# Attention scores of two heads in the row halves of the PE array, with the mask as matmuls of its own

## The chip, the cores and the metric

The kernel runs on one core of a Trainium2 chip. The metric is the device time of one execution in microseconds (us). Kernels are compared with runs of the kernel before on the same chip.

Names used below: PE is the TensorE (matmuls and transposes), PEld the loading of its weights, PSUM the memory that it writes its results to, ACT the ScalarE, DVE the VectorE, POOL the GpSimd. A "pair" is two heads of one batch; there are 4 batches of 4 pairs.

## The reference, cut to what matters

```python
# q, k, v: (4, 8, 768, 64); float32
k_rep = k.reshape(B, H, 12, 64, 64).mean(axis=3)       # 12 key blocks of 64
gate  = einsum('bhsd,bhnd->bhsn', q, k_rep)            # future blocks: -1e9
top   = the 3 best blocks of each query, plus its own block
scores = where(mask by block & causal, q @ k.T / 8, -1e9)
attn   = softmax(scores) @ v
x      = attn, heads side by side                      # (3072, 512)
out    = gelu_tanh(x @ w_in) @ w_out                   # 512 -> 2048 -> 512
```

So per batch there is an attention stage (scores, exp, values) and an MLP of two layers. Most of the arithmetic is in the MLP.

## The kernel before

The kernel lists its operations with estimated durations and priorities. A small list scheduler in it fixes one order for each engine when the kernel is built. The order is static: it does not change when an instruction is late on the chip. 110 "filler" matmuls of zeros with the lowest priority stand where this plan sees the PE idle.

The block mask is folded into the score matmul. Each head has a query tile of 76 rows: 64 rows of q, then 12 rows that say which key blocks are shut. The key tile has 12 rows in which row n is a large number over the columns of block n. One matmul over 76 rows gives score plus mask:

```python
# before, cut; i: buffer of the pair, h: head of the pair
def kc(a, h):                        # one copy per head: to rows 0 to 63
    copy(eng, kT16[i][h][0:64, a * HALF:(a + 1) * HALF],
         plan.buf["wk", p, a][64 * h:64 * h + 64, 0:HALF])
...
def mask(_):                         # mask, transposed: 64 columns = 2 heads x 32
    for c in range(1, NC):
        nc.tensor.transpose(mk16[0:64, c * 128:(c + 1) * 128],
            madd[i][:, 2 * (c - 1):2 * c, :].rearrange("p a b -> p (a b)"), ident16)
def mc(h):                           # one copy per head: to rows 64 to 75
    copy(eng, qT16[i][h][64:76, 128:S], ...[32 * h:32 * h + 12, 128:S])
...
groups = [(0, 5), (1, 4), (2, 3)]    # key chunks; 896 score columns in a unit
for h in range(2):
    for gi, (ja, jb) in enumerate(groups):
        # scores into one of two PSUM tiles "wide" of 1024 columns
        nc.tensor.matmul(st[:, x:e], kT16[i][h][0:76, s0:s0 + 128],
                         qT16[i][h][0:76, ...], start=True, stop=True)
        # exp of 896 columns on ACT -> at; causal triangle on POOL
        # values: 7 matmuls of 65 columns: at (128 x 128) x [v | 1]
```

Then follow the division by the row sum (DVE), a transpose (PE), and the MLP: line 629 is its first layer (512 and 256 columns at a time), line 659 its second (512 columns). The second layer of a batch is spread over the attention stage of the next batch: the static order puts its matmuls between score and value matmuls so that the PE need not wait for the exps.

The softmax here doesn't subtract the row's maximum and nothing guards it: scores larger than these inputs give would overflow.

## Time and profile before

| | us |
|---|---|
| time, median of 2 runs | 294.15 |
| span of the profiled execution | 291.4 |
| first matmul of the MLP starts | 49.8 |
| last matmul of batch 0's first MLP layer starts | 76.0 |
| last MLP matmul starts | 287.2 |

First the head of the page: the span and the busy time of each engine.

```profile
span 291.4 us, 5960 instructions
PE 279.3 (96%) x2330; PEld 173.8 (60%) x2330; DVE 144.0 (49%) x448; ACT 191.5 (66%) x252; POOL 48.0 (16%) x119
```

The PE is nearest to its span, but the ends of matmuls in this profile are modelled, so "busy" alone proves little. The Trainium skill says the same ("Perfetto Trace Analysis" has the TensorE profile time as "a model, not a measurement"). What is recorded is the start of every matmul, and the distance from one start to the next is what the first of the two cost. In this trace these distances are nearly always 29 to 36 ns for 65 columns, 55 or 56 for 128, 108 to 110 for 256 and 215 to 220 for 512. From about 50 us on there is hardly anything else: the PE is packed, and every nanosecond that it saves or loses there goes to the total time. (TensorE: Matmul & The Clock Gate, "Wait — 56ns, not 53.3ns?", gives 55.6 and 215.7 ns for 128 and 512 columns; this trace agrees.)

Next the busy time of the engines in four stretches: up to the first MLP matmul, batch 0's first MLP layer, everything to the last MLP matmul, and the end.

```profile
core 0: us, PE busy (x) PEld busy (x) DVE busy (x) ACT busy (x) POOL busy (x), PEclk, DMA share, GB/s
0.00:49.80 49.80, 43.90 (x466) 34.12 (x467) 34.98 (x126) 34.25 (x51) 16.94 (x46) 1.00 1.13 191
49.80:76.10 26.30, 25.23 (x176) 16.07 (x174) 11.75 (x38) 16.23 (x22) 0.41 (x1) 1.00 1.17 171
76.10:287.20 211.10, 209.81 (x1693) 123.65 (x1691) 97.31 (x287) 140.46 (x179) 30.69 (x72) 1.00 0.37 73
287.20:291.40 4.20, 0.37 (x2) 0.00 (x0) 0.00 (x0) 0.58 (x1) 0.00 (x0) 0.98 0.17 62
```

The first stretch is different from the rest: there 108 of the 110 fillers run, so the PE has room, and ACT and DVE carry the copies. In the third stretch the PE is busy for 209.8 of 211.1 us.

Two pieces of the PE's timeline in the packed part, in the order start, length, engine, line, operation. One is a stretch of an attention stage (L533 scores, L571 values, L659 second MLP layer). The other is the first MLP layer (L629) with mask transposes (L472) in between.

```profile
91.40 0.55 PE L533 MATMUL wide_85<-qT_0_116,kT_0_118 76*128 76x512 f16 x3
91.78 0.38 PE L571 MATMUL bank_88<-v_114,at_1_1_1443 128*128 128x65 f16 x7
92.00 0.38 PE L659 MATMUL bank_89<-w_out_103,gT_986 128*128 128x512 f16 x1
92.22 0.55 PE L533 MATMUL wide_86<-qT_0_116,kT_0_118 76*128 76x512 f16 x3
...
136.28 0.49 PE L629 MATMUL wide_86<-xT_1428,w_in_102 128*128 128x512 f16 x2
136.70 0.47 PE L472 MATMUL bank_88<-ident_96,madd_121 128*64 128x128 f16 x5
137.10 0.71 PE L629 MATMUL wide_86<-xT_1428,w_in_102 128*128 128x512 f16 x3
```

Read the starts. The 896 score columns take 91.78 - 91.40 = 0.38 us, just their columns; the 76-row scores stand between 128-row matmuls without any gap. The mask transposes do not fit so well. Two MLP matmuls (512 and 256 columns, 0.325 us) should end 0.325 us after 136.28, but L472 starts after 0.42 us. Five transposes of 128 columns (0.28 us) take 0.40 us (24 ns of the difference lie between the first two of them). Their weights are 64 columns wide (128\*64 in the line), all others are 128 wide. So each change of tile width costs about 95 ns here, and about 110 ns with what the matmul after it loses.

### The profile page before, as it was taken

Reading aid. Unit: us, or ns where it says so; the run is one execution under the profiler, and the core shown is the slowest. Engines: PE = TensorE matmul, PEld = TensorE weight load, DVE = VectorE, ACT = ScalarE, POOL = GpSimd, SP = SyncE. Lnnn points to the kernel's source line nnn. Section 1 sums busy time; section 2 is a strip of 40 time slices with the busy share of each in tenths; the row PEclk is TensorE's granted clock in tenths of the full one; section 3 lists DMA queues with packets and bytes.
Section 4 is the critical chain, followed back from the end, with each engine's and each line's share of the span. In section 5 each row is a group of like instructions: output and inputs, shape, how many; then the busy total and the mean of one; then the engine's idle time right before and its main releaser. Section 6 shows DMA issues by size and latency. Waiting matters only on the chain.

```text
span 291.4 us, 5960 instructions
## 1 busy us (share of the span) xinstructions
PE 279.3 (96%) x2330; PEld 173.8 (60%) x2330; DVE 144.0 (49%) x448; ACT 191.5 (66%) x252; POOL 48.0 (16%) x119
## 2 busy tenths in 40 slices
PE   7998899899999999999999999999999999999994
PEld 6776667575666655656646665666557644665441
DVE  4787873138578878673676978850024410000000
ACT  3667869557799695676789976376799921664111
POOL 7023224000043220000024430000034400000000
PEclk9999999999999999999999999999999999999999
DMA  9999999999999966865822110200000101100111
GB/s 171 219 213 197 190 171 174 199 170 146 168 159 175 163 133 146 177 127 97 128 43 64 58 38 37 74 0 0 2 36 2 40 36 72 38 0 2 72 72 72
DMA packets 115836, 29.75 MB, mean 102 GB/s; under 512 B 110176, under 2 KB 112224, under 8 KB 115808
## 3 DMA queue, kind: packets, MB, share of 16 engines
q1 hardware_dynamic: 113216, 25.18, 47.7%
q0 software_dynamic: 2592, 4.19, 8.4%
q8 instruction: 18, 0.29, 0.4%
q14 instruction: 10, 0.08, 0.1%
HBM read 27.26 MB, written 6.29 MB: 115 GB/s over the span
## 4 chain that ended last, share of the span: by engine, by line
PE 80%; ACT 13%; DVE 3%; issue 2%; POOL 1%; ACTq 0%; DVEq 0%
PE wide_86 L629 14%; PE wide_85 L629 14%; PE bank_88 L659 7%; PE bank_87 L659 7%; PE bank_90 L659 6%; PE bank_89 L659 6%; PE wide_85 L533 5%; PE wide_86 L533 4%; PE bank_89 L430 3%; PE bank_90 L571 2%; PE bank_89 L571 1%; PE bank_90 L430 1%; PE bank_88 L430 1%; PE bank_87 L571 1%; PE bank_88 L600 1%
## 5 line engine op out<-in xcount | busy, mean ns | idle before, releaser
L629 PEld LDWEIGHTS <-w_in_102 128*128 128x128 f16 x512 | 49.7, 99 | 34.0 <-issue 1.8
L659 PEld LDWEIGHTS <-gT_3446 128*128 128x128 f16 x96 | 9.4, 98 | 11.2
L659 PEld LDWEIGHTS <-gT_2781 128*128 128x128 f16 x96 | 9.1, 97 | 8.0
L694 PEld LDWEIGHTS <-z 128*128 128x128 f16 x110 | 10.9, 105 | 4.2 <-DVE bmask L164 1.3
L659 PEld LDWEIGHTS <-gT_1883 128*128 128x128 f16 x96 | 8.8, 98 | 7.6
L629 PE MATMUL wide_85<-xT_555,w_in_102 128*128 128x512 f16 x64 | 12.4, 326 | 1.0 <-ACT gT_986 L642 0.6
L629 PE MATMUL wide_86<-xT_1428,w_in_102 128*128 128x512 f16 x64 | 12.4, 326 | 0.2 <-ACT gT_1883 L642 0.2
L659 PEld LDWEIGHTS <-gT_986 128*128 128x128 f16 x96 | 8.5, 98 | 6.7
L629 PE MATMUL wide_85<-xT_3108,w_in_102 128*128 128x512 f16 x64 | 12.2, 326 | 0.0
L629 PE MATMUL wide_86<-xT_555,w_in_102 128*128 128x512 f16 x64 | 12.2, 326 | 0.0
L629 PE MATMUL wide_86<-xT_2319,w_in_102 128*128 128x512 f16 x64 | 12.0, 326 | 0.0
L629 PE MATMUL wide_85<-xT_2319,w_in_102 128*128 128x512 f16 x64 | 11.9, 326 | 0.0
L629 PE MATMUL wide_86<-xT_3108,w_in_102 128*128 128x512 f16 x64 | 11.7, 326 | 0.0
L629 PE MATMUL wide_85<-xT_1428,w_in_102 128*128 128x512 f16 x64 | 11.7, 326 | 0.0
L504 ACT ACT_TABLE_LOAD x8 | 10.3, 1283 | 0.9 <-PEq L746 0.8
L642 ACT ACTIVATE gT_986<-wide_85 128x768 f16<-128x768 f32 x8 | 6.5, 810 | 5.2 <-PE wide_85 L629 5.2
L190 DVE COPY osb_0_3000<-bank_89 128x512 f32<-128x512 f32 x1 | 0.7, 692 | 18.4 <-PE bank_89 L659 18.4
L659 PE MATMUL bank_90<-w_out_103,gT_2781 128*128 128x512 f16 x32 | 9.7, 379 | 0.0
L642 ACT ACTIVATE gT_986<-wide_86 128x768 f16<-128x768 f32 x8 | 6.5, 808 | 4.6 <-PE wide_86 L629 4.6
L694 PE MATMUL bank_88<-z 128*128 128x256 f16 x33 | 8.9, 290 | 0.3 <-ACT kT_1_107 L188 0.3
L642 ACT ACTIVATE gT_2781<-wide_86 128x768 f16<-128x768 f32 x8 | 6.5, 810 | 3.8 <-PE wide_86 L629 3.8
L642 ACT ACTIVATE gT_3446<-wide_86 128x768 f16<-128x768 f32 x8 | 6.5, 810 | 3.7 <-PE wide_86 L629 3.7
(947 smaller groups left out, 697.4 us busy)
## 6 DMA issues: line engine op xcount, KB each, us to landing
w_in_102<-in_moe_w_in_dram POOLq DMA_DIRECT2D x1, 2048.0 KB, 14.3
w_out_103<-in_moe_w_out_dram POOLq DMA_DIRECT2D x1, 2048.0 KB, 17.3
k_sd_135<-in_k_dram SPq DMA_DIRECT2D x2, 192.0 KB, 3.0
q_sd_142<-in_q_dram SPq DMA_DIRECT2D x2, 192.0 KB, 3.7
v_sd_147<-in_v_dram SPq DMA_DIRECT2D x2, 192.0 KB, 4.3
k_sd_152<-in_k_dram SPq DMA_DIRECT2D x2, 192.0 KB, 4.6
q_sd_157<-in_q_dram SPq DMA_DIRECT2D x2, 192.0 KB, 4.6
v_sd_162<-in_v_dram SPq DMA_DIRECT2D x2, 192.0 KB, 4.5
```

What stands on the lines that cost most here:

```text
L190: nc.vector.tensor_copy(out=out, in_=in_)
L430: nc.tensor.matmul(gt[:, (c - 1) * 24:c * 24], T["qT32", p][:, c * 128:(c + 1) * 128], T["ksb", p].rearrange("p h n -> p (h n)"), start=Tr ...
L504: nc.scalar.activation(out=t, in_=bmask[:, 0, 0:1], func=AF.Exp if key[0] == "exp" else AF.Gelu_apprx_tanh, bias=0.0, scale=1.0)
L533: nc.tensor.matmul(st[:, x:e], kT16[i][h][0:76, s0:s0 + 128], qT16[i][h][0:76, s0 + (x - cb):s0 + (e - cb)], start=True, stop=True)
L571: nc.tensor.matmul(pvv[:, qc, 0:65], at[:, cb + (qc - jc) * 128: cb + (qc - jc + 1) * 128], v16[i][:, jc, h, :], start=(gi == 0 and jc == ...
L600: nc.tensor.transpose(oT16[:, c * 128:(c + 1) * 128], T["xn", p][:, c].rearrange("p h d -> p (h d)"), ident16)
L629: nc.tensor.matmul(hps[:, u:e], w_in16[:, ci, f * 128:(f + 1) * 128], T["xT", b][:, ci, u:e], start=(ci == 0), stop=(ci == HP - 1))
L642: nc.scalar.activation(out=T["gT", b][:, f, :], in_=plan.buf["hps", b, f][:, 0:S], func=AF.Gelu_apprx_tanh, bias=0.0, scale=1.0)
L659: nc.tensor.matmul(plan.buf["ops", b, ti], T["gT", b][:, f, ti * 128:(ti + 1) * 128], w_out16[:, f, :], start=(f == 0), stop=(f == NF - 1))
L694: nc.tensor.matmul(plan.buf["warm", n][:, 0:256], z[:, 0:128], z[:, 0:256], start=True, stop=True)
```

## The change

The intent: the array has 128 rows, and a score needs 64. So the scores of the two heads go to the two row halves, to run at the same time. The mask no longer fits into the rows and becomes separate matmuls of 12 rows. These accumulate onto the scores, two at a time in batch 0 and four at a time (two heads of two units) in batches 1 to 3, in row groups of 32. One unit holds both heads, 512 columns each. Copies of k, q and mask become one for both heads. The core of the diff, cut:

```diff
-    bank = [psum.tile([128, 512], FP32, name=f"bank_{i}") for i in range(4)]
+    both = [psum.tile([128, 1024], FP32, name="both")]          # values of both heads
+    bank = [psum.tile([128, 512], FP32, name=f"bank_{i}") for i in range(2)]
...
-        def kc(a, h):
+        def kc(a):
             def emit(eng):
-                copy(eng, kT16[i][h][0:64, a * HALF:(a + 1) * HALF],
-                     plan.buf["wk", p, a][64 * h:64 * h + 64, 0:HALF])
+                copy(eng, kT16[i][:, a * HALF:(a + 1) * HALF],
+                     plan.buf["wk", p, a][:, 0:HALF])
...                                       # q and mask copies likewise; mask into mT16
-                    mk16[0:64, c * 128:(c + 1) * 128],
-                    madd[i][:, 2 * (c - 1):2 * c, :].rearrange(
-                        "p a b -> p (a b)"), ident16)
+                    mk16[:, c * 128:(c + 1) * 128],              # now 128 columns wide
+                    madd[i][:, 2 * (c - 1):2 * c].rearrange(
+                        "p h z n -> p (h z n)"), ident16)
...
+    units = [[(0, 0, 512)], [(0, 512, 256), (4, 512, 256)],     # key chunk, query, width
+             [(1, 128, 512)], [(1, 640, 128), (3, 384, 384)],
+             [(2, 256, 512)], [(5, 640, 128)]]
...
-                            nc.tensor.matmul(
-                                st[:, x:e], kT16[i][h][0:76, s0:s0 + 128],
-                                qT16[i][h][0:76, ...], start=True, stop=True)
+                for j, q0, w in pieces:
+                    for h in range(2):
+                        r = slice(64 * h, 64 * h + 64)
+                        nc.tensor.matmul(
+                            st[:, 512 * h + x:512 * h + x + w],
+                            kT16[i][r, j * 128:(j + 1) * 128],
+                            qT16[i][r, q0:q0 + w],
+                            start=x == 0, stop=False, skip_group_check=True)
...
+            if b and ui % 2 == 0:
+                continue
+            group = (ui - 1, ui) if b else (ui,)
...
+                for _x, z, h, j, lo, w, at in sorted(work):      # the mask matmuls
+                    r = 64 * h + 32 * z
+                    nc.tensor.matmul(
+                        plan.buf["st", p, group[z]][
+                            :, 512 * h + at:512 * h + at + w],
+                        T["E16"][r:r + 12, j * 128:(j + 1) * 128],
+                        mT16[i][r:r + 12, lo:lo + w],
+                        start=False, stop=True, skip_group_check=True)
...                                       # exp, triangle and values of both heads in one unit
```

More of the change, by code (lines that the diff above doesn't have):

```diff
@@ L168 @@
     w_out16 = persist.tile([128, NF, DM], FP16)
-    qT16, kT16, v16, madd = [], [], [], []
+    qT16, kT16, mT16, v16, madd = [], [], [], [], []
     for i in range(NB):
-        qT16.append([persist.tile([128, S], FP16, name=f"qT_{i}_{h}")
-                     for h in range(2)])
-        kT16.append([persist.tile([128, S], FP16, name=f"kT_{i}_{h}")
-                     for h in range(2)])
+        qT16.append(persist.tile([128, S], FP16, name=f"qT_{i}"))
+        kT16.append(persist.tile([128, S], FP16, name=f"kT_{i}"))
+        mT16.append(persist.tile([128, S], FP16, name=f"mT_{i}"))
         v16.append(persist.tile([128, NC, 2, 65], FP16, name=f"v_{i}"))
-        madd.append(persist.tile([128, NG, 32], FP16, name=f"madd_{i}"))
+        madd.append(persist.tile([128, NG, 2, 32], FP16, name=f"madd_{i}"))
     plan = Plan({
-        "wide": (wide, 2), "pre": (bank, 2), "pv": (bank, 2), "ops": (bank, 1),
+        "wide": (wide, 2), "pre": (bank, 2), "pv": (both, 1), "ops": (bank, 1),
     })
@@ L251, in e16, with e16_more @@
         def e16(_):
-            T["E16"] = const.tile([12, S], FP16, name="E16")
-            E16 = T["E16"]
-            nc.gpsimd.memset(E16, MASKVAL)
+            T["E16"] = E16 = const.tile([128, S], FP16, name="E16")
+            nc.gpsimd.memset(E16[0:12], MASKVAL)
             nc.gpsimd.affine_select(
-                out=E16.rearrange("p (n w) -> p n w", w=64),
-                in_=E16.rearrange("p (n w) -> p n w", w=64),
+                out=E16[0:12].rearrange("p (n w) -> p n w", w=64),
+                in_=E16[0:12].rearrange("p (n w) -> p n w", w=64),
                 compare_op=ALU.is_equal, fill=0.0,
                 base=0, pattern=[[1, NBLK], [0, 64]], channel_multiplier=-1)
-        c_E["E"] = add({POOL: 2.0}, e16, [], prio=-50)
+        e0 = add({POOL: 2.0}, e16, [], prio=-50)
+        def e16_more(_):
+            for r in range(1, 4):
+                nc.vector.tensor_copy(out=T["E16"][32 * r:32 * r + 12],
+                                      in_=T["E16"][0:12])
+        c_E["E"] = add({DVE: 0.9}, e16_more, [e0], prio=-20)
         def gates(_):
@@ L282, in fill @@
         def fill(i):
-            def emit(_):
-                for h in range(2):
-                    nc.vector.tensor_copy(out=kT16[i][h][64:76, :],
-                                          in_=T["E16"])
-                    nc.vector.memset(qT16[i][h][64:76, 0:128], 0.0)
-            c_E["fill", i] = add({DVE: 0.8}, emit, [c_E["E"]],
-                                 prio=100 * i - 30)
             def emit_p(_):
@@ L296, in consts @@
             fill(i)
-    groups = [(0, 5), (1, 4), (2, 3)]
     last = {}
@@ L360, in pre, with kc_all @@
             ksr.append(add({DVE: 0.83}, ks_all, [t], pr))
-            def kc_all(h):
-                def emit(eng):
-                    copy(eng, kT16[i][h][0:64, :],
-                         T["kT32", p][64 * h:64 * h + 64, :])
-                return emit
-            kcs = [add({DVE: 0.47, ACT: 0.7}, kc_all(h),
-                       [t, old.get("k", None)], pr + 0.1) for h in range(2)]
+            def kc_all(eng):
+                copy(eng, kT16[i], T["kT32", p])
+            kcs = [add({DVE: 0.47, ACT: 0.7}, kc_all,
+                       [t, old.get("k", None)], pr + 0.1)]
         for a in range(0 if by_dve(p) else 2):
@@ L376, in pre @@
             ksr.append(r)
-            c0 = add({DVE: 0.47, ACT: 0.38}, kc(a, 0),
-                     [t, old.get("k", None)], pr)
-            c1 = add({DVE: 0.47, ACT: 0.38}, kc(a, 1),
-                     [t, old.get("k", None)], pr)
-            kcs += [c0, c1]
-            add({"NONE": 0.0}, lambda _: None, [r, c0, c1], pr,
+            c = add({DVE: 0.47, ACT: 0.38}, kc(a), [t, old.get("k", None)], pr)
+            kcs.append(c)
+            add({"NONE": 0.0}, lambda _: None, [r, c], pr,
                 gives=[("wk", p, a)])
@@ L455, in sel_e, with q16 @@
                 in1=mx8[:, :, 2:3].to_broadcast([128, NG, NBLK]), op=ALU.is_ge)
-            nc.vector.scalar_tensor_tensor(
-                out=madd[i][:, :, 0:NBLK], in0=sel, scalar=-1.0,
-                in1=T["ownm1"], op0=ALU.add, op1=ALU.max)
-        sel = add({DVE: 1.55}, sel_e, [gm, c_E["ones", i]], pr)
-        def q16(h):
-            def emit(eng):
-                copy(eng, qT16[i][h][0:64, :],
-                     T["qT32", p][h * 64:(h + 1) * 64, :])
-            return emit
-        q16s = [add({DVE: 0.47, ACT: 0.7}, q16(h), qcs + [old.get("s")],
-                    pr + 0.1) for h in range(2)]
+            for z in range(2):
+                nc.vector.scalar_tensor_tensor(
+                    out=madd[i][:, :, z, 0:NBLK], in0=sel, scalar=-1.0,
+                    in1=T["ownm1"], op0=ALU.add, op1=ALU.max)
+        sel = add({DVE: 1.7}, sel_e, [gm, c_E["ones", i]], pr)
+        def q16(eng):
+            copy(eng, qT16[i], T["qT32", p])
+        q16s = [add({DVE: 0.47, ACT: 0.7}, q16, qcs + [old.get("s")],
+                    pr + 0.1)]
         def mask(_):
@@ L472, in mask, with mc @@
                 nc.tensor.transpose(
-                    mk16[0:64, c * 128:(c + 1) * 128],
-                    madd[i][:, 2 * (c - 1):2 * c, :].rearrange(
-                        "p a b -> p (a b)"), ident16)
+                    mk16[:, c * 128:(c + 1) * 128],
+                    madd[i][:, 2 * (c - 1):2 * c].rearrange(
+                        "p h z n -> p (h z n)"), ident16)
         m = add({PE: 0.27 * slow}, mask, [sel], pr, takes=("pre", ("mk", p)))
-        def mc(h):
-            def emit(eng):
-                copy(eng, qT16[i][h][64:76, 128:S],
-                     plan.buf["mk", p].bitcast(FP16)[
-                         32 * h:32 * h + 12, 128:S])
-            return emit
-        mcs = [add({DVE: 0.4, ACT: 0.6}, mc(h), [m, old.get("s")], pr)
-               for h in range(2)]
+        def mc(eng):
+            copy(eng, mT16[i][:, 128:S],
+                 plan.buf["mk", p].bitcast(FP16)[:, 128:S])
+        mcs = [add({DVE: 0.4, ACT: 0.6}, mc, [m, old.get("s")], pr)]
         add({"NONE": 0.0}, lambda _: None, mcs, pr, gives=[("mk", p)])
-        rdy[p] = [kcs[0::2] + [q16s[0], mcs[0], c_E["fill", i]],
-                  kcs[1::2] + [q16s[1], mcs[1], c_E["fill", i]]]
+        rdy[p] = (kcs + q16s, mcs + [c_E["E"]])
         last.setdefault(p, {})["pre"] = add(
@@ L516, in heads @@
         norms = []
-        for h in range(2):
-            pvs = []
-            for gi, (ja, jb) in enumerate(groups):
-                u = (p, h, gi)
-                pr = base + 10 * (3 * h + gi)
-                wa = S - ja * 128
-                wb = S - jb * 128
-                def st_e(_, u=u, ja=ja, jb=jb, wa=wa, wb=wb, h=h):
-                    st = plan.buf[("st",) + u]
-                    for jc, cb in ((ja, 0), (jb, wa)):
-                        s0 = jc * 128
-                        w = S - s0
-                        x = cb
-                        while x < cb + w:
-                            e = min(cb + w, (x // 512 + 1) * 512)
-                            nc.tensor.matmul(
-                                st[:, x:e], kT16[i][h][0:76, s0:s0 + 128],
-                                qT16[i][h][0:76,
-                                           s0 + (x - cb):s0 + (e - cb)],
-                                start=True, stop=True)
-                            x = e
-                st = add({PE: 0.375 * slow}, st_e, rdy[p][h], pr,
-                         takes=("wide", ("st",) + u))
-                def ex_e(_, u=u, n=wa + wb):
-                    T["at", u] = atp.tile([128, 896], FP16, tag="at",
-                                          name="at_%d_%d_%d" % u)
@@ new lines, in heads, with st_e, mm_e, ex_e @@
+        pvs = []
+        sts = {}
+        for ui, pieces in enumerate(units):
+            u = (p, ui)
+            pr = base + 10 * ui
+            def st_e(_, u=u, pieces=pieces):
+                st = plan.buf[("st",) + u]
+                x = 0
+                for j, q0, w in pieces:
[6 more added lines that the diff above has]
+                            start=x == 0, stop=False, skip_group_check=True)
+                    x += w
+            sts[ui] = add({PE: 0.225 if ui < 5 else 0.07}, st_e,
+                          rdy[p][0] + gelus.get(b - 1, [])[NF - 2:NF - 1],
+                          pr, takes=("wide", ("st",) + u))
+            if b and ui % 2 == 0:
+                continue
+            group = (ui - 1, ui) if b else (ui,)
+            def mm_e(_, group=group):
+                work = []
+                for z, y in enumerate(group):
+                    x = 0
+                    for j, q0, w in units[y]:
+                        lo = max(q0, 128)
+                        for h in range(2):
+                            work.append((x, z, h, j, lo, q0 + w - lo,
+                                         x + lo - q0))
+                        x += w
+                for _x, z, h, j, lo, w, at in sorted(work):
[6 more added lines that the diff above has]
+                        start=False, stop=True, skip_group_check=True)
+            mm = add({PE: 0.235}, mm_e, [sts[y] for y in group] + rdy[p][1],
+                     pr)
+            for ui, pieces in ((y, units[y]) for y in group):
+                u = (p, ui)
+                pr = base + 10 * ui
+                n = sum(w for _, _, w in pieces)
+                diag = [sum(w for _, _, w in pieces[:x])
+                        for x, (j, q0, _) in enumerate(pieces) if q0 == 128 * j]
+                def ex_e(_, u=u, n=n):
+                    at = atp.tile([128, 2, 512], FP16, tag="at",
+                                  name="at_%d_%d" % u)
+                    T["at", u] = at
@@ L545, in ex_e @@
                     nc.scalar.activation(
-                        out=T["at", u][:, 0:n],
-                        in_=plan.buf[("st",) + u][:, 0:n],
+                        out=at[:, :, 0:n],
+                        in_=plan.buf[("st",) + u].rearrange(
+                            "p (h w) -> p h w", h=2)[:, :, 0:n],
                         func=AF.Exp, bias=0.0, scale=SCALE)
-                ex = add({ACT: 0.8}, ex_e,
-                         [st, table(("exp", b), gelus.get(b - 1, []), base)],
-                         pr,
-                         gives=[("st",) + u])
+                ex = add({ACT: 0.91 if n > 128 else 0.33}, ex_e,
+                         [mm, table(("exp", b), gelus.get(b - 1, []), base)],
+                         pr, gives=[("st",) + u])
@@ L553, in heads, with af_e @@
                 exps.setdefault(b, []).append(ex)
-                def af_e(_, u=u, wa=wa):
-                    at = T["at", u]
-                    dg = bass.AP(at.tensor, at.offset,
-                                 [at.ap[0], [wa, 2], [1, 128]])
+                def af_e(_, u=u, c=diag[0]):
+                    dg = T["at", u][:, :, c:c + 128]
                     nc.gpsimd.affine_select(
@@ L563, in heads, with pv_e @@
                 af = add({POOL: 0.36}, af_e, [ex], pr)
-                def pv_e(_, u=u, ja=ja, jb=jb, wa=wa, h=h, gi=gi):
-                    pvv = plan.buf["pv", p, h][:, 0:NC * 66].rearrange(
-                        "p (c w) -> p c w", w=66)
-                    at = T["at", u]
-                    for jc, cb in ((ja, 0), (jb, wa)):
-                        for qc in range(jc, NC):
-                            nc.tensor.matmul(
-                                pvv[:, qc, 0:65],
-                                at[:, cb + (qc - jc) * 128:
-                                   cb + (qc - jc + 1) * 128],
-                                v16[i][:, jc, h, :],
-                                start=(gi == 0 and jc == 0 and qc == 0),
-                                stop=(gi == 2 and jc == jb and qc == NC - 1),
-                                skip_group_check=True)
-                pvs.append(add({PE: 0.2 * slow}, pv_e,
+                def pv_e(_, u=u, pieces=pieces):
+                    for h in range(2):
+                        pvv = plan.buf["pv", p][:, 512 * h:512 * h + NC * 66].rearrange(
+                            "p (c w) -> p c w", w=66)
+                        x = 0
+                        for j, q0, w in pieces:
+                            for c in range(q0 // 128, (q0 + w) // 128):
+                                nc.tensor.matmul(
+                                    pvv[:, c, 0:65],
+                                    T["at", u][:, h, x:x + 128],
+                                    v16[i][:, j, h, :],
+                                    start=u[1] == 0 and x == 0,
+                                    stop=u[1] == 5,
+                                    skip_group_check=True)
+                                x += 128
+                pvs.append(add({PE: 0.061 * (n // 128)}, pv_e,
                                [af, ld["v16", p], c_E["ones", i]] + pvs[-1:],
-                               pr, takes=("pv", ("pv", p, h))))
+                               pr, takes=("pv", ("pv", p))))
+        for h in range(2):
             def zr_e(_, h=h):
-                pvv = plan.buf["pv", p, h][:, 0:NC * 66].rearrange(
+                pvv = plan.buf["pv", p][:, 512 * h:512 * h + NC * 66].rearrange(
                     "p (c w) -> p c w", w=66)
@@ L593, in zr_e @@
                     in1=zr.to_broadcast([128, NC, 64]), op=ALU.mult)
-            norms.append(add({DVE: 0.7}, zr_e, pvs, base - 20,
-                             gives=[("pv", p, h)]))
+            norms.append(add({DVE: 0.7}, zr_e, pvs[-1:], base - 20))
+        add({"NONE": 0.0}, lambda _: None, norms, base, gives=[("pv", p)])
         def ot_e(_):
@@ L615, in heads @@
         last.setdefault(p, {}).update(
-            {"k": st, "s": st, "v": pvs[-1]})
+            {"k": mm, "s": mm, "v": pvs[-1]})
     out_rows = out.rearrange("(n p) c -> n p c", p=128)
```

## The prediction

> **What bounds the kernel now.** TensorE. The busy row gives PE 279.3 of 291.4 us, ACT 191.5, DVE 144.0. A busy PE is modelled, so I checked the starts of successive matmuls: from 51 us on, each starts 29 to 31 ns (65 columns), 109 (256) or 216 ns (512) after the one before it, nearly all of them, so from there to the last output the PE stands packed. Only 0 to 51 us is different: there the chain of waits mixes ACT copies, DVE copies and exps, 110 filler matmuls (L694) show PE has room, ACT is busy 27.8 and DVE 25.6 of the 36 us from 15 to 51.
>
> **Removed.** (1) Scores L533: per pair 2 x 2688 columns, one head after the other, 37.3 us by start distances (28.1 after 51 us). With two heads in the two row halves the 16 matmuls should take half, about 1.12 us a pair instead of 2.33. (2) Copies: k, q and mask copies become one for both heads: three fewer per pair at 0.47 to 0.7 us on ACT or DVE, and the fills of the constant rows (eight copies, eight memsets on DVE at the start). (3) Mask transposes L472 go from 64 to 128 columns. In the old trace they show what a change of tile shape costs: 512-column matmul to L472 309 ns instead of 216, and L472 to the next 152 instead of 56, so about 95 ns each way; 16 visits, about 200 ns each.
>
> **Added.** 256 mask matmuls of 12 rows with their weight loads; in batches 1 to 3 four run at once, 3 x 512 columns a pair = 0.65 us; in batch 0 two at once, 1.1 us. And changes of tile shape: 128, 64 and 32 rows alternate. In the new instruction order I count 67 changes before the first MLP matmul and 185 after it. The Trainium skill ("TensorEngine Tiling (Array Packing)", Key Properties) says changing the tiling mode drains the TensorE; the 95 ns above agrees for columns; no run shows rows yet.
>
> **Sum.** Batch 0: ACT and DVE lose about 4 us each; first MLP matmul about 5 us earlier (w_in lands near 43 us, so not before that). After it, PE packed: scores and masks -12 x 0.5 = -6, transposes -2.4, changes 185 x D. D = 95 ns: +17.6, net about +9, total about 299; D = 50: about 290; D = 0: about 281. Exp time stays (5 x 0.92 + 0.28 against 6 x 0.815 us a pair), but a unit pair waits for one mask group, which leaves ACT gaps of about 1 us a group; PE filler of the previous batch (L659, 20.7 us) should hide most: +1 to 2 us. I think D near that of columns likeliest, but a shorter one possible.
>
> Predicted 295 us, range 283 to 303; faster by over 2% 0.34, within 2% 0.42, slower 0.24.
>
> **What the profile would show.** Start distances in pairs of score matmuls of the two heads: a few ns, then 216 ns for 512 columns; if they stand 216 apart, the halves do not overlap. At each change of tile shape an excess over columns/2.4 GHz: that is D. First L-MLP matmul at 45 to 47 us. About 96 fewer copies in all on ACT and DVE less 16 more mask operations. In the last attention stage (209 to 228 us before), ACT with gaps and PE filled.
>
> **What would make it wrong.** D small (then 281 to 286); row halves not concurrent (then over 305); PE order standing still for the mask group because ACT or a PSUM buffer is late, in place of packed; batch 0 bound by the loads or by the gate chain so that the copies give nothing.

## The result, and the profile after

The changed kernel took 303.44 us (median of 2 runs, 303.18 to 303.7) against 294.15 us. The ratio is 1.0316, with a 95% interval of 1.0271 to 1.036. A second comparison with more runs, on another occasion, gave 303.55 against 293.39 us, ratio 1.035 (1.033 to 1.037). It is slower by a little over 3%. Ratios here and below are the mean time of one kernel's fast runs over that of the other's of the same rounds, so not quite the ratio of the quoted medians. The prediction (295 us, range 283 to 303) missed: it held a faster or an equal kernel for likelier, and the change is clearly slower. (The profiled execution of the kernel before took 293.12 us, 1.0 us less than its median; so the spans below differ by 10.6 us and the medians by 9.3.)

The head of the page of the changed kernel:

```profile
span 302.0 us, 6413 instructions
PE 295.2 (98%) x2586; PEld 169.1 (56%) x2586; DVE 132.7 (44%) x430; ACT 173.6 (57%) x220; POOL 48.7 (16%) x119
```

Its busy time in the same four stretches, each bounded by the same matmuls as before, with the same columns:

```profile
0.00:48.60 48.60, 44.13 (x482) 30.12 (x483) 32.05 (x115) 28.51 (x38) 18.49 (x47) 1.00 1.11 189
48.60:73.60 25.00, 24.91 (x174) 15.86 (x170) 9.59 (x35) 15.19 (x20) 0.07 (x1) 1.00 1.20 175
73.60:297.10 223.50, 222.60 (x1910) 120.40 (x1909) 91.09 (x284) 129.34 (x162) 30.18 (x72) 1.00 0.37 71
297.10:302.00 4.90, 3.53 (x30) 2.67 (x28) 0.00 (x0) 0.58 (x1) 0.00 (x0) 1.00 0.14 54
```

ACT fell by 17.9 us and DVE by 11.3 us, as intended, and little came of it. The first two stretches together are 2.5 us shorter (73.6 against 76.1). The third is 12.4 us longer, with the PE still packed (222.6 of 223.5 us), and the end is 0.7 us longer. That makes 10.6 us of span.

Here is the stretch of an attention stage to set beside the one of before (L519 scores, L545 masks, L589 values, L618 transposes, L677 second MLP layer):

```profile
88.81 0.38 PE L677 MATMUL bank_89<-w_out_102,gT_997 128*128 128x512 f16 x1
89.12 0.39 PE L519 MATMUL wide_86<-qT_108,kT_109 64*128 64x128 f16 x4
89.44 0.42 PE L589 MATMUL both<-v_111,at_0_1365 128*128 128x65 f16 x8
89.70 0.41 PE L589 MATMUL both<-v_111,at_1_1393 128*128 128x65 f16 x8
89.95 0.50 PE L618 MATMUL bank_88<-ident_95,xn_1354 128*128 128x128 f16 x6
90.38 0.39 PE L545 MATMUL wide_85<-mT_110,E_127 12*128 12x512 f16 x2
90.39 0.39 PE L545 MATMUL wide_86<-mT_110,E_127 12*128 12x128 f16 x4
90.71 0.60 PE L677 MATMUL bank_89<-w_out_102,gT_997 128*128 128x512 f16 x2
```

The overlap works. Four score matmuls (128 and 384 columns, for two heads) start at 89.12 and the next work at 89.44, 0.32 us later; one after the other, their 1024 columns would take 0.44 us. The six mask matmuls (two times 512, 128 and 384 columns) take 0.33 us in place of 0.87. In the records the two heads of a piece start 3 to 4 ns apart, and the four masks within 10 ns. The Trainium skill gives "Δstart ≤4ns" for tiles in distinct row groups (TensorE: Matmul & The Clock Gate, "Why this matters for your kernels"); this trace agrees.

But each of these runs of matmuls also costs a gap ahead of it and behind it. 512 columns from 88.81 should end 0.216 us later; the scores start 0.31 us later. The scores' own 512 columns take 0.32 us until the values start, not 0.216. The transposes at 89.95 take 0.43 us instead of 0.33. The tile heights in these lines are 128, 64, 128, 12 (a 32-row tile), 128, and at every change about 95 ns are lost. Counting all changes after the first MLP matmul in the trace, by the excess of the start distance over the columns' time:

| change of tile height | count | median excess, ns |
|---|---|---|
| 128 to 64 | 69 | 96 |
| 64 to 128 | 44 | 103 |
| 32 to 128 | 36 | 91 |
| 64 to 32 | 25 | 93 |
| 128 to 32 | 11 | 100 |

185 changes at these medians are 17.9 us. The Trainium skill says that changing the tiling mode drains the TensorE (TensorEngine Tiling (Array Packing), "Key Properties"), that is, empties it first. The gaps fit a drain. The page gives no size. The records of the weight loads (PEld) show one thing more. First the changed kernel at two changes, then the kernel before where the height stays the same:

```profile
115.39 0.10 PEld L519 LDWEIGHTS <-kT_119 64*128 64x128 f16 x2 [0.42 <-issue]
115.39 0.39 PE L519 MATMUL wide_85<-qT_118,kT_119 64*128 64x512 f16 x2
115.71 0.10 PEld L677 LDWEIGHTS <-gT_997 128*128 128x128 f16 x1 [0.23 <-issue]
115.71 0.39 PE L677 MATMUL bank_89<-w_out_102,gT_997 128*128 128x512 f16 x1
...
213.78 0.38 PE L659 MATMUL bank_89<-w_out_103,gT_2781 128*128 128x512 f16 x1
213.78 0.53 PEld L533 LDWEIGHTS <-kT_1_107 76*128 76x128 f16 x3
213.99 0.55 PE L533 MATMUL wide_86<-qT_1_105,kT_1_107 76*128 76x512 f16 x3
```

Where the height stays, the load of the next weights starts together with the matmul before (213.78), 0.21 us ahead of its own matmul. At a change it does not: in 184 of the 185 changes it starts 4 or 5 ns ahead of its own matmul, after the gap. So a change also ends the loading ahead. Whether the 95 ns are the emptying of the array or something that the late load brings with it, no run here separates; the price is the same.

The third stretch can be settled line by line. Each distance from one start to the next is charged to the first of the two matmuls:

| matmuls of the third stretch | before, us | after, us |
|---|---|---|
| scores | 28.1 | 21.0 |
| masks | - | 11.8 |
| values | 15.8 | 17.5 |
| second MLP layer | 85.3 | 87.3 |
| fillers | - | 3.9 |
| all else (first MLP layer, gates, transposes) | 82.0 | 81.9 |
| sum | 211.2 | 223.5 |

The gaps can be taken out of these sums. A change costs a little more than the table of medians says, because the matmul after it is also some 10 ns slower (226 ns for 512 columns in place of 216): 107 ns in the mean. Beside the changes there are waits, here an excess of more than 60 ns over the column time without a change of shape, or what at a change goes well beyond the price of one. The kernel before has waits too, which is easily forgotten:

| in the third stretch | before, us | after, us | difference |
|---|---|---|---|
| scores and masks by their column times | 27.4 | 21.5 | -5.8 |
| changes of width (before, 22) or height (after, 185) | 2.4 | 19.7 | +17.3 |
| waits, and the column time of the fillers in them | 2.7 | 1.6 + 3.1 | +2.0 |
| all else | 178.7 | 177.6 | -1.1 |

These make the measured +12.3 us. Of the -1.1, -0.6 are three matmuls of the second MLP layer that now run in the second stretch. The overlap gained 5.8 us, and the changes of tile height, 19.7 us, more than ate it.

### The profile page after: what moved, and what is told of

The parts are those of the page before. It is cut to its first block, busy times and chain, and to the rows that moved or that the text cites. A ratio compares the mean times of both kernels' runs of the same rounds, so it can differ in the third digit from the quotient of the medians.

```text
span 302.0 us, 6413 instructions
## 1 busy us (share of the span) xinstructions
PE 295.2 (98%) x2586; PEld 169.1 (56%) x2586; DVE 132.7 (44%) x430; ACT 173.6 (57%) x220; POOL 48.7 (16%) x119
## 4 chain that ended last, share of the span: by engine, by line
PE 93%; DVE 3%; ACT 2%; issue 1%; ACTq 0%; DVEq 0%
PE bank_89 L677 17%; PE wide_85 L647 14%; PE wide_86 L647 13%; PE bank_88 L677 12%; PE both L589 7%; PE wide_85 L519 5%; PE wide_86 L519 4%; PE bank_88 L421 3%; PE wide_85 L545 3%; PE bank_89 L421 2%; PE bank_89 L712 2%; PE bank_88 L712 2%; PE wide_86 L545 2%; PE bank_88 L618 1%; PE bank_89 L618 1%
## 5 line engine op out<-in xcount | busy, mean ns | idle before, releaser
L647 PEld LDWEIGHTS <-w_in_101 128*128 128x128 f16 x512 | 49.6, 99 | 31.4 <-issue 0.6
L677 PE MATMUL bank_89<-w_out_102,gT_1948 128*128 128x512 f16 x64 | 18.8, 381 | 0.0
L677 PE MATMUL bank_89<-w_out_102,gT_997 128*128 128x512 f16 x64 | 17.2, 381 | 0.0
L712 PE MATMUL bank_89<-z 128*128 128x256 f16 x57 | 14.5, 293 | 1.5 <-DVE osb_5_1870 L190 0.5
L677 PEld LDWEIGHTS <-gT_3618 128*128 128x128 f16 x96 | 9.4, 98 | 11.2
L712 PE MATMUL bank_88<-z 128*128 128x256 f16 x53 | 13.5, 295 | 1.9 <-DVE bmask L165 1.3
L677 PE MATMUL bank_88<-w_out_102,gT_2860 128*128 128x512 f16 x48 | 13.8, 381 | 0.0
L677 PEld LDWEIGHTS <-gT_1948 128*128 128x128 f16 x96 | 8.3, 98 | 9.5 <-issue 4.2
L677 PEld LDWEIGHTS <-gT_2860 128*128 128x128 f16 x96 | 8.3, 98 | 9.3 <-issue 4.0
L677 PEld LDWEIGHTS <-gT_997 128*128 128x128 f16 x96 | 8.1, 98 | 9.5 <-issue 4.0
L677 PE MATMUL bank_89<-w_out_102,gT_2860 128*128 128x512 f16 x48 | 13.1, 381 | 0.0
L647 PE MATMUL wide_86<-xT_1443,w_in_101 128*128 128x512 f16 x64 | 12.2, 326 | 0.0
L647 PE MATMUL wide_86<-xT_517,w_in_101 128*128 128x512 f16 x64 | 12.2, 326 | 0.0
L647 PE MATMUL wide_85<-xT_1443,w_in_101 128*128 128x512 f16 x64 | 12.2, 326 | 0.0
L647 PE MATMUL wide_86<-xT_2421,w_in_101 128*128 128x512 f16 x64 | 12.0, 326 | 0.0
L647 PE MATMUL wide_85<-xT_517,w_in_101 128*128 128x512 f16 x64 | 11.9, 326 | 0.1
L647 PE MATMUL wide_86<-xT_3236,w_in_101 128*128 128x512 f16 x64 | 11.9, 326 | 0.0
L647 PE MATMUL wide_85<-xT_3236,w_in_101 128*128 128x512 f16 x64 | 11.9, 326 | 0.0
L647 PE MATMUL wide_85<-xT_2421,w_in_101 128*128 128x512 f16 x64 | 11.9, 326 | 0.0
L545 PEld LDWEIGHTS <-E_127 12*128 12x128 f16 x256 | 6.8, 91 | 8.3 <-issue 5.8
```

Of the source, the lines that this page charges most:

```text
L545: nc.tensor.matmul(plan.buf["st", p, group[z]][:, 512 * h + at:512 * h + at + w], T["E16"][r:r + 12, j * 128:(j + 1) * 128], mT16[i][r:r + ...
L647: nc.tensor.matmul(hps[:, u:e], w_in16[:, ci, f * 128:(f + 1) * 128], T["xT", b][:, ci, u:e], start=(ci == 0), stop=(ci == HP - 1))
L677: nc.tensor.matmul(plan.buf["ops", b, ti], T["gT", b][:, f, ti * 128:(ti + 1) * 128], w_out16[:, f, :], start=(f == 0), stop=(f == NF - 1))
L712: nc.tensor.matmul(plan.buf["warm", n][:, 0:256], z[:, 0:128], z[:, 0:256], start=True, stop=True)
```

## The experiments

My theory after this: the changes of tile height drain the PE at 95 to 100 ns each, and there are enough of them to turn a gain into a loss. Rivals: the gaps are waits for ACT or PSUM that only look like drains; the halves do not really overlap; left-over fillers make the loss; batch 0 is bound by something that the change does not touch.

### The cost of a change by itself, in the kernel before

Three kernels add one small matmul to each of the 72 score units of batches 1 to 3 in the kernel before. Only its number of rows differs.

```diff
                     st = plan.buf[("st",) + u]
+                    if b:
+                        nc.tensor.matmul(            # overwritten by the scores
+                            st[:, 0:64], kT16[i][h][0:64, 0:128],
+                            qT16[i][h][0:64, 0:64],
+                            start=True, stop=True)   # or rows 0:76, or rows 64:76
```

> The kernel before with one extra 64-row, 64-column matmul ahead of each of the 72 score units of batches 1 to 3, in the midst of full-height matmuls; its output is overwritten, the result stays right. Theory (each change of tile height drains the PE, about 95 ns): 72 x (29 + 2 x 95) ns = +15.8 us, about 310 us. Rival (changes of row height are free, the changed kernel lost its time in waits and order): 72 x 29 ns = +2 us, about 296 us.

> Control: the same extra matmul, but over 76 rows, so no change of tile height. Both theories: 72 x 29 ns = +2 us, about 296 us. If it costs as much as the 64-row probe, the probe itself and not the change of height is dear.

> The same extra matmul over the 12 mask rows (partitions 64 to 75), so a 32-row tile. Theory: as the 64-row probe, +15.8 us, about 310 us. If the drain depends on the height of the tile: clearly less than the 64-row probe. Rival: +2 us.

Measured against 293.33 us of the kernel before: 64 rows 308.42 us (ratio 1.051, 1.0487 to 1.0534), 76 rows 295.46 us (1.0069, 1.0049 to 1.0089), 12 rows 308.62 us (1.051, 1.0487 to 1.0533). The timeline of the PE around one such matmul (L664 second MLP layer, L528 the probe, L538 scores), first with 64 rows:

```profile
90.59 0.38 PE L664 MATMUL bank<-w_out,gT 128*128 128x512 f16 x1
90.91 0.20 PE L528 MATMUL wide<-qT,kT 64*128 64x64 f16 x1
91.04 0.56 PE L538 MATMUL wide<-qT,kT 76*128 76x512 f16 x3
```

The same place in the timeline of the 76-row control:

```profile
89.31 0.38 PE L664 MATMUL bank<-w_out,gT 128*128 128x512 f16 x1
89.52 0.20 PE L528 MATMUL wide<-qT,kT 76*128 76x64 f16 x1
89.56 0.54 PE L538 MATMUL wide<-qT,kT 76*128 76x512 f16 x3
```

With 76 rows the 512-column matmul is followed after 0.21 us, the probe after 0.04 us. With 64 rows these are 0.32 and 0.13 us. The same work at another tile height costs about 13 us more over 72 places, or 90 ns for each of the 144 changes, and the height (64 or 32 rows) does not matter. (By the start distances each change costs about 105 ns here, too; some 1.4 us of that is hidden, as the waits of the third stretch fall from 2.3 us with 76 rows to 0.9 us with 64.) 76 rows count as the full height. The probe stands in the kernel before, with its order and its PSUM use, so waits of the changed kernel have no part in it. The rival that changes of row height are free falls.

### The width changes that the kernel before already paid for

The mask transposes of the kernel before read 64 columns. This run lets them read 128, the next mask chunk's columns included; the upper 64 output rows are not used.

```diff
-        madd.append(persist.tile([128, NG, 32], FP16, name=f"madd_{i}"))
+        madd.append(persist.tile([128, NG + 2, 32], FP16, name=f"madd_{i}"))
...
-                    mk16[0:64, c * 128:(c + 1) * 128],
-                    madd[i][:, 2 * (c - 1):2 * c, :].rearrange(
+                    mk16[:, c * 128:(c + 1) * 128],
+                    madd[i][:, 2 * (c - 1):2 * c + 2, :].rearrange(
```

> The kernel before with its mask transposes reading 128 columns in place of 64 (the upper 64 output rows are not used), which undoes the 32 changes of column width. Theory (excesses read in its trace of 94 + 24 ns going in, 96 + 11 ns coming out, 12 visits in the packed part): -2.7 us, about 291.4 us. Rival (such gaps are hidden, another wait takes their place): no change.

> The wide transposes alone again, on the chip of the mixtures, to compare with them: 0.992 of the time before, about 291.5 us.

Measured: 290.99 against 293.33 us, ratio 0.992 (0.9903 to 0.9938); on a second occasion 291.11 against 293.28 us, 0.9924 (0.9904 to 0.9945). That is 2.2 to 2.3 us, a little less than the 2.7 expected; in both traces the third stretch takes 209.1 in place of 211.2 us. Five transposes in the midst of the first MLP layer now take 0.28 us, just their columns (compare the last three lines of the fence of before):

```profile
135.26 1.46 PE L629 MATMUL wide<-xT,w_in 128*128 128x512 f16 x8
136.56 0.44 PE L472 MATMUL bank<-ident,madd 128*128 128x128 f16 x5
136.84 2.00 PE L629 MATMUL wide<-xT,w_in 128*128 128x512 f16 x11
```

The result is right. This small edit beats both kernels, the one before by 0.8% (a small gain, but the interval leaves out 1) and the changed one by about 4%, and nothing with right results in this study is faster beyond the noise.

### What the overlap is worth

Both heads' scores in the same rows, so that they cannot overlap; order and changes of height stay.

```diff
-                        r = slice(64 * h, 64 * h + 64)
+                        r = slice(0, 64)          # second run: only "if b"
```

> Wrong result on purpose: the changed kernel with both heads' scores in rows 0 to 63, so that the two heads cannot overlap; order and changes of height stay. Theory (two halves run at once, worth half the score time): 12 x 1.12 = +13.4 us in the packed part and 0 to +4.5 us in batch 0: 317 to 321 us. Rival (the halves do not truly overlap): no change.

> Wrong scores on purpose: as the one-half run, but only batches 1 to 3 put both heads into rows 0 to 63; batch 0 stays as changed. The one-half run came to 341 us with its TensorE clock granted at half from about 10 to 60 us, so it does not price the overlap. Theory: 12 x 1.12 = +13.4 us, about 317 us with the clock at 1.0. If the overlap were worth less: below +10 us.

The first run took 341.02 us, far over the expectation, and its clock tells why it can't be used. The row of granted clock in 40 slices, from the page of this run:

```profile
PEclk9965555599999999999999999999999999999999
```

The same row from the page of the kernel before:

```profile
PEclk9999999999999999999999999999999999999999
```

In slices 3 to 8 the clock was granted at 0.5 to 0.6; why it fell is not shown. The second run, with the change in batches 1 to 3 alone, kept it at 1.0 from 49 us on and took 317.51 us: 14 us more than the changed kernel, where 13.4 were expected. The third stretch of its trace is the cleaner measure:

```profile
74.40:311.20 236.80, 235.90 (x1910) 124.66 (x1909) 90.44 (x284) 129.78 (x162) 30.10 (x72) 1.00 0.35 67
```

It takes 236.8 us (236.9 from the starts of its first and last matmul) against 223.5 of the changed kernel, 13.4 us more, just as expected; and the first run, whose clock was back at full speed by then, also takes 236.9 us there. So the halves do run at once, and the overlap is worth what the columns say. It is not the reason for the loss. (With these inputs the scores hardly matter beside the mask, so comparison does not guard the scores.)

### The masks taken away

```diff
-                for _x, z, h, j, lo, w, at in sorted(work):
+                for _x, z, h, j, lo, w, at in ([] if b else sorted(work)):
```

> Wrong result on purpose: the changed kernel without the mask matmuls of batches 1 to 3. Changes of height after the first MLP matmul go from 185 to 138. Theory: 12 x 0.65 us of mask time and 47 changes at 97 ns: -7.8 - 4.6 = -12.4 us, about 291 us. If changes cost nothing: -7.8 us, about 295.6 us. If exps were bound by the wait for the masks: more than -12.4 us.

Measured: 291.34 us, against 294.16 us of the kernel before on that chip (0.9918, 0.9892 to 0.9944), wrong result as intended. Theory said about 291, a rival without a cost of changes 295.6. In the trace the third stretch is 12.6 us shorter than the changed kernel's (210.9 us), where 12.4 were expected. This also bounds the whole idea: even with masks in batches 1 to 3 for nothing, the scores in halves end where the wide transposes alone do: 138 changes of height remain, 14.7 us by the start distances.

### Masks at the height of the scores

Mask rows padded with zeros to 64 rows: one tile height less to change between, but two at a time rather than four.

```diff
+            nc.vector.memset(E16, 0.0)
             nc.gpsimd.memset(E16[0:12], MASKVAL)
...
-                    r = 64 * h + 32 * z
+                    r = 64 * h
-                        T["E16"][r:r + 12, j * 128:(j + 1) * 128],
-                        mT16[i][r:r + 12, lo:lo + w],
+                        T["E16"][r:r + 64, j * 128:(j + 1) * 128],
+                        mT16[i][r:r + 64, lo:lo + w],
```

> The changed kernel with the mask matmuls over 64 rows (12 used, the rest zeros) so that scores and masks share one tile height, two at a time instead of four. Changes of height go from 185 to 160 after the first MLP matmul and from 67 to 52 before. Theory: masks of batches 1 to 3 take 12 x 0.43 us more (+5.1), 25 changes at 97 ns fewer (-2.4), some of the 15 in batch 0 (-0 to -1.4): +1 to +3 us, 304.5 to 306.5 us. If the four-way overlap of masks is worth nothing: -2.4 to -4 us.

Measured: 304.37 us (ratio 1.0358, 1.0332 to 1.0385), 0.9 us over the changed kernel by medians, a little under the expected range. In the trace the third stretch is 2.3 us longer than the changed kernel's (225.8 against 223.5), where +5.1 - 2.4 = +2.7 was expected. Batch 0, however, came out 1.8 us shorter (71.8 against 73.5 us), more than the 0 to 1.4 that I had allowed. That led to the next pair of runs.

### Batch 0: the same masks there alone

In batch 0 the masks run two at a time anyway, so 64 rows cost nothing there and take away 15 of the 67 changes ahead of the first MLP matmul.

> The changed kernel with 64-row mask matmuls (zeros beyond the 12 mask rows) in batch 0 alone, where they run two at a time anyway: no matmul gets longer, but the changes of height before the first MLP matmul go from 67 to 52; batches 1 to 3 keep 185. Theory (in batch 0, too, these changes lie on the chain and eat what the fewer copies give): 15 x 97 ns = -1.5 us, the end of batch 0's first MLP layer from 73.5 to about 72 us, the whole about 301.9 us. Rival (batch 0 is bound by loads, copies or the gate chain, and PE has room for the changes): no change, 303.4 us.

> The changed kernel unaltered, to have it on one chip with the next run. 1.0316 of the time before, as in the first comparison, within 0.3%.

> The same kernel as the 64-row masks in batch 0 alone, on one chip with the changed kernel. Theory: 1.5 to 1.8 us less than it (ratio lower by 0.005 to 0.006), batch 0's first MLP layer ending at about 72 us. Rival: the same as it.

Measured: first 302.43 us (1.0305, 1.0286 to 1.0323). Then, on one chip with the changed kernel: 302.49 us (1.0303, 1.0285 to 1.0321) beside 303.55 us (1.035, 1.033 to 1.037). That is 1.1 us less by medians, 1.4 us by the difference of ratios (one of the five runs of the changed kernel is 1.0 us above its median), under the 1.5 to 1.8 expected; the five times of each do not overlap. (The changed kernel's ratio itself came 0.33% over that of the first comparison, just outside the 0.3% expected.) In the profiled executions of the two the third stretch is the same 223.5 us; the last matmul of batch 0's first MLP layer starts at 71.8 and 72.4 us where the changed kernel has 73.5 and 73.1. One such reading proves little: in the six profiles of the kernel before, of its probes and of its wide transposes it lies between 75.7 and 77.0 us. The times on one chip carry the argument: in batch 0 too the changes of height lie on the chain. They are one reason why the fewer copies gave less than expected; 67 of them at 97 ns would be 6.5 us. That all of the missing gain went this way is not shown: only 15 were taken away.

### Fewer fillers

```diff
-        for n in range(110):
+        for n in range(50):
```

> The changed kernel with 50 filler matmuls in place of 110. In its trace 50 of 110 start before the first MLP matmul, about 31 in the packed part at 109 ns each and 28 after the last useful matmul. Theory (the plan puts left-over fillers into gaps that the real PE does not have): -3.4 us in the packed part and up to -1 us at the end, about 299 to 300 us. Rival (fillers stand only in true gaps): no change, 303.4 us.

Measured: 302.27 us (1.0286, 1.0261 to 1.0311), about 1.2 us under the changed kernel and not 3.4 to 4.4. The trace says why I was wrong. The end is 0.7 us shorter, but the third stretch only 0.8 us (222.7 instead of 223.5), half of it because four changes of height went with the fillers. The fillers there, 3.9 us by start distance, had mostly stood in true gaps, and with them gone the PE waits. One such place is the end of batch 1 in this run, where the first MLP layer waits for the last pair's output (L618 transposes, L188 copy, L647 MLP):

```profile
119.52 0.51 PE L618 MATMUL bank<-ident,xn 128*128 128x128 f16 x6 [0.28 <-DVE xn L609]
120.06 0.80 ACT L188 COPY xT<-bank 128x768 f16<-128x768 f16 x1 [0.98 <-PE bank L618]
120.91 0.48 PE L647 MATMUL wide<-xT,w_in 128*128 128x512 f16 x2 [0.89 <-ACT xT L188]
```

In this run the waits of the third stretch sum to 4.1 us, the longest of them at the ends of batches, for DVE and ACT. But the kernel before had waits of 2.7 us in its third stretch. So new waits and fillers are 1.4 us of the loss in this run and 2.0 us in the changed kernel, beside the 17.3 us of the changes of shape. A reading of the waits at the ends of batches that fits, not tested: with both heads in one unit, both divisions of a pair come after its last unit, and at a batch's end nothing of the second MLP layer is left to cover them.

### A mixture: batch 0 as changed, the rest as before with wide transposes

Batch 0 had gained, so it was put together with the wide transposes. The edit is long; in short:

```diff
+        joint = b == 0                 # one copy for k, q and mask in batch 0
...
+        if b == 0:
+            return heads_joint(p)      # row halves, 12-row masks, both heads in a unit
```

> A mixture: batch 0 as in the changed kernel (row halves, both heads in one unit, one copy for two heads), batches 1 to 3 as before (76 rows, no change of height) with the 128-column mask transposes. Theory: the changed kernel's earlier first MLP matmul (48.6 against 51.0 us, -2.4) and the transposes (-2.3 to -2.7) add up: 288.5 to 290 us. Rival (batch 0 gains nothing by itself, or its gain is eaten later): 291 us, as the wide transposes alone.

> The mixture with 50 fillers instead of 110. Theory: left-over fillers beyond batch 0 cost little, 0 to -1.5 us against the mixture.

Measured: 291.04 us (0.992, 0.9899 to 0.9941), the same as the wide transposes alone (291.11 on that chip): the mixture gains nothing on top. (The 51.0 us in the expectation is the misreading that is told of below; the first MLP matmul of before starts at 49.8.) Its batch 0 ends its first MLP layer at 76.6 us, not at 73.5. The mixture has to write the constant mask rows for the later batches in that time and has another order; which of these took the gain was not tried. With 50 fillers it was worse, 294.5 us in the median of its four fast runs (1.0015, 0.9983 to 1.0046; 292.7 to 295.0 us; two more runs, near 298 us, were slow), where 0 to 1.5 us less than the mixture had been expected. Again the clock row shows something, here of a fast run; what made the clock fall is not shown:

```profile
PEclk9987996899999999999999999999999999999999
```

## Why the prediction was wrong

**Its reading of what bounds the kernel held.** The PE was packed before and after, and what ACT and DVE lost (17.9 and 11.3 us of busy time) gave little: 2.5 us up to the end of batch 0's first MLP layer. One number was misread: the prediction took the PE to be packed from about 51 us on, near where the chain of waits first shows an MLP matmul (51.35); the first one starts at 49.8. The change brought it to 48.6, not to "45 to 47".

**The overlap held.** Predicted -6 us, -5.8 by the column times; the two one-half runs confirm it for the scores (+13.4 us each in the third stretch without it).

**The step that failed is the weight given to D, the cost of a change of tile height.** The prediction counted 185 changes, read 95 ns per change of width in the old trace, and put the sum with D = 95 ns at "about 299". Then it wrote "D near that of columns likeliest, but a shorter one possible" and moved to 295, which by its own three sums stands for a D of about 75 ns, with a third of the chances on "faster". The measured D is 91 to 103 ns at the change itself for every sort of change, 107 ns with the slower matmul after it, and the probes in the kernel before give 90 ns net. Nothing in the trace had supported a shorter one.

**Even the sum with D = 95 was low.** Of its terms, batch 0, the changes of height and the end were mis-sized (measured in the two profiled executions):

| term | predicted, us | measured, us |
|---|---|---|
| batch 0 to the end of its first MLP layer | -5 | -2.5 |
| overlap of scores and masks, packed part | -6 | -5.8 |
| 185 changes of height | +17.6 at D = 95 | +19.7 |
| changes of width gone | -2.4 | -2.4 |
| new gaps and fillers, packed part | +1 to +2 | +2.0 |
| the end | 0 | +0.7 |

The four terms of the packed part sum to 13.5; the -1.1 us of "all else" above makes that the measured 12.3. For batch 0 I counted copies only, though I had counted its 67 changes in the same text; they got no cost, because fillers ran there. The runs with 64-row masks in batch 0 show that they are not harmless: 15 fewer gave 1.1 to 1.4 us. At the end, 28 left-over fillers run after the last useful matmul.

**The warnings.** "PE order standing still" was foreseen for the mask groups; what came were waits at the ends of batches, and with the fillers they are 2.0 us, as large as the "+1 to 2" of the sum. "Row halves not concurrent" did not happen. A D above 95 ns was not among the warnings.

## What to carry to other kernels

Before splitting the array into row tiles, count the changes of tile shape in the order that the engine will run, not the columns saved: here 512 columns saved were worth 0.21 us and a run of tiled matmuls between full-height ones cost about 0.2 us in its two changes. By these numbers row tiling pays only where one run of tiled matmuls saves clearly more than 512 columns (an estimate; no run here tried long ones), and a matmul of 76 rows that rides along at full height can beat two that are each smaller. When an old trace already shows the price of an effect in a sister case, predict with that price and don't average it with a hope; and look for the same effect in what you already have, since undoing it there (128-column transposes) was the gain to be had.

## What the Trainium skill lacked or had wrong

- TensorEngine Tiling (Array Packing), "Key Properties", says that a mode switch drains but not how long: here 91 to 103 ns (medians) for every change between 128, 64 and 32 rows, and 93 to 96 ns between 128 and 64 columns, at full clock. "Performance Considerations" there lists an overhead per matmul but not this one.
- The same page gives tiles of 128, 64 and 32 rows, but does not say outright what a matmul of a height between them counts as: 76 rows ran without a gap beside 128 rows (0.04 us for a 64-column probe against 0.13 us at 64 rows). Nor does it say that all changes cost alike: 12 rows cost as much as 64 (308.62 and 308.42 us).
- No page says what a change of mode does to weight loads. Here the load for the matmul after a change starts 4 or 5 ns before that matmul (184 of 185 changes), where at one height most start 1 or 2 ns after the start of the matmul before.
- TensorE: Matmul & The Clock Gate, Part 3, says that weight loads overlap running matmuls only where the row group differs, though its text on the mechanism also allows for a background weight buffer. Here the records show a load starting 2 ns after a matmul in the same rows had started (before, 128 rows, and in the one-half run, 64 rows), and matmuls of equal rows follow each other at their column time (216 ns for 512 columns).
- Its Part 1 ties the clock to how busy the PE has recently been. Here two edits in batch 0 let the clock fall to about half for some 50 us (one-half run), or to 0.6 in one slice of 7 us (mixture with 50 fillers), while the PE row of the page showed 80% or more busy in all of those slices; the busy row, whose ends are modelled, did not warn, and the cause stays open.
